# A delta-rule recurrence with a hardswish MLP behind it: eleven quarter products from block four on, and loads spread one a unit

## The chip, the cores and the metric

One core of a Trainium2 chip runs the whole kernel. The metric is the device time of one execution in microseconds (us). Five engines work side by side on the core: TensorE (PE, with its weight loads PEld), VectorE (DVE), ScalarE (ACT), GpSimd (POOL), and SyncE (SP), whose queue issues nearly all DMA transfers, in order, to the DMA engines. Each engine runs its own instructions in the order in which they were written and waits at semaphores for the others.

## The reference

Batch 4, 8 heads, 768 tokens, head width 48. A recurrence over the tokens (the delta rule) is followed by a two-layer MLP on 3072 tokens of width 384, with 2048 features in between:

```python
k_n = k / (np.linalg.norm(k, axis=-1, keepdims=True) + 1e-06)
for t in range(S):
    y[:, :, t] = q[:, :, t] @ state
    v_old = state^T @ k_n[:, :, t]
    state += beta[t] * outer(k_n[:, :, t], v[:, :, t] - v_old)
x = y.transpose(0, 2, 1, 3).reshape(B * S, H * D)
h = x @ w_in
g = h * np.clip(h + 3.0, 0.0, 6.0) / 6.0
out = g @ w_out
```

(the loop body is written here in short; all is float32).

## The kernel before

**The recurrence** is done in 24 chunks `t` of 32 tokens, for all batches and heads at once. For a chunk, `prep(t)` (from L505 on) scales the keys, turns keys and queries over on TensorE (`pt`, L524), evicts them into `KQ` (L532), and multiplies them with each other (`sc`, L547). The inverses of small triangular matrices are made in groups of four chunks on VectorE (L759 and L764). `chain(t)` multiplies with the state (`ks`, L806), then `pz` and `py` (L827) and the state's update `su` (L938), and hands the chunk's output over, turned (`yt`, L873, evicted to `xT` at L877). Keys go through `kf` (four chunks a tile, two tiles), queries through four buffers `qb`, values through two buffers `vf`. The norms of a group's keys need one square a chunk (`sq`, L409) and a reduction of it (L413).

**The MLP** works on blocks `blk` of two chunks, 256 rows, so there are twelve, 0 to 11. The up stage multiplies a block with `w_in`, the down stage the result `g` with `w_out`. `mlp_units` (L1286) gives the order: the down stage of a block, then the up stage of the next one. There are two ways to do an up stage. `up` (L982) does, for each of 16 groups of 128 features, three matmuls of 256 columns, which are twelve quarter products for each pair of groups (L994), followed by a relu on ACT (L1001) and a product on DVE (L1004). `up_by_eleven` (L1059) gets the eight quarter products of two thirds of the width from seven, by sums of weights and of tokens in the manner of Strassen and Winograd, and does the last third directly: eleven quarter products for a pair `j`, as nine matmuls (L1066) in `begin(j)` and `end(j)`. A pair also has an early eviction by ACT (L1080) with two additions on POOL (L1030), two on DVE (L1093 and L1097), a last copy (L1100), the relu (L1104) and the product (L1107). The relu writes into a tile named `o` that has one buffer. The down stage puts its results into the same `o`; from block 2 on it is `down_by_seven` (L1199, matmuls at L1218, sums of `g` at L1204, additions of results at L1228 on POOL and DVE). A block's results leave by eight stores (`to_dram`, L1143) on SP's queue.

`up_by_eleven` needs sums of `w_in` that are made once, in place of one part of it: `weight_sums` (L1032), sixteen operations on POOL, recorded two a step during the down stage of block `UF - 1`. It needs four sums of a block's tokens as well: `token_sums` (L1048), on DVE.

**The order.** A matmul in float32 leaves two records in the profile. The first chunks and the first units of the MLP follow an order written out by hand (`ORDER`; it holds the loads of chunks 0 to 11 of q, 0 to 16 of k and 0 to 5 of v). From chunk 5 on a loop does the rest: each chunk has 15 units, and in each unit come the pieces of `chain` and `prep` that `plan` names for it, then loads, then one unit of the MLP (`take(units)`), then a share of the inverses (`take(fill, ...)`). So two chunks hold the 14 units of a down stage and the 16 of an up stage; an up stage begins in unit 12 of an odd chunk. The loads of the loop are four of v at a chunk's start, four of q in its unit 2, and those of k (sixteen for four chunks), two a unit from the third chunk of a group on. `behind_tensor` (L1407) adds to an instruction a wait for the last TensorE instruction recorded so far; before, only words of `ORDER` use it.

Of the kernel before, what the change touches and what calls it, by code (L numbers as in the profile page):

```python
# [44 lines left out]
def kernel(  # L45
# [21 lines left out]
    nc = tc.nc  # L67
# [33 lines left out]
    def group(t):  # L101
        return (0, t) if t < G0 else ((t - G0) // GS + 1, (t - G0) % GS)
# [873 lines left out]
    def settle(n=0, name="u"):  # L976

        relu(name)
        while len(pending[name]) > n:
            pending[name].pop(0)()  # L980
# [34 lines left out]
                past.add(("up", blk))  # L1015
            yield

    UF = 5
    S1, S2, S4 = (sums_in[:, i] for i in range(3))

    def w_tiles(s, i):
# [10 lines left out]
    def weight_sums():  # L1032
        for j in range(0, NPR, 2):
            r = slice(j, j + 2)
            plus_minus(S1[:, r], W21[:, r], W22[:, r], ALU.add)
            yield
            plus_minus(S2[:, r], S1[:, r], W11[:, r], ALU.subtract)
            yield
            plus_minus(S4[:, r], W12[:, r], S2[:, r], ALU.subtract)
            yield  # L1040
            plus_minus(W21[:, r], W11[:, r], W21[:, r], ALU.subtract)
            yield
# [5 lines left out]
    def token_sums(blk):  # L1048
        if blk < UF or ("seam", blk * CB + 1) not in past:
            return  # L1050
        needs(("seam", blk * CB), ("seam", blk * CB + 1), ("up", blk - 1))
        B11, B12, B21, B22, _, _ = (
            x.rearrange("p (a b) -> p a b", b=16) for x in x_tiles(blk)
        )
        for out, a, b in ((T1x, B12, B11), (T2x, B22, T1x), (B12, B22, B12), (T4x, B21, T2x)):
            nc.vector.tensor_tensor(out=out, in0=a, in1=b, op=ALU.subtract)
        past.add(("sums", blk))
# [228 lines left out]
    def mlp_units():  # L1286
# [10 lines left out]
        def downs(blk):  # L1297
            if blk >= FIRST:
                yield from down_by_seven(blk)
                return  # L1300
            for c in range(CB):
                for f in range(0, NFC, WF):
                    if c == 0:
                        needs(*(("read", ("ph", blk, f + i, None)) for i in range(2)))
                    down(blk, c, f)
                    yield

        for blk in range(1, N // CB):
            mode["of"] = "down"
            mode["mean"] = 0.72 if blk + 1 < UF else 0.4  # L1310
            sums = weight_sums() if blk == UF - 1 else iter(())
            for _ in downs(blk):
# [3 lines left out]
            if blk + 1 < N // CB:  # L1316
                mode["of"] = "eleven" if blk + 1 >= UF else "up"
                for n, _ in enumerate((up_by_eleven if blk + 1 >= UF else up)(blk + 1)):
                    if blk + 1 == FIRST and n >= HF:
# [10 lines left out]
    def take(gen, n=1):  # L1330
        for _ in range(n):
            while next(gen, None) == 1:
                pass
# [6 lines left out]
    gens = {}  # L1340

    def made(name, make, ok=True):
        if name not in gens:
            gens[name] = make() if ok else iter(())
        return gens[name]

    def prep_of(t):
        return made(("p", t), lambda: prep(t), t < N)

    def chain_of(t):  # L1350
        return made(("h", t), lambda: chain(t))
# [4 lines left out]
    def inverse_of(g):  # L1356
        return made(
            ("i", g), lambda: halves_of(g) if g == 1 else inverse(g), g < NG
        )

    def keys_of(g):
        return made(
            ("k", g), lambda: chained(*(load_k(first(g) + i) for i in range(size(g)))), g < NG
        )
# [42 lines left out]
    def behind_tensor(ins):  # L1407
        last = next(
            i for i in reversed(nc.cur_bb.bb.instructions) if i.engine == mybir.EngineType.PE
        )  # L1410
        tc.add_manual_dep(
            ins, last.name,
            mybir.DependencyInfo(mybir.DependencyClass.Sync, mybir.DependencyReason.DATA),
            reason="held back",
        )

    def do(word):
        if word in ("K", "Q", "V", "W"):
            n = len(nc.cur_bb.bb.instructions)
            next(gens[word.lower()])  # L1420
            (new,) = nc.cur_bb.bb.instructions[n:]
            behind_tensor(new)
        elif word in gens:
            next(gens[word])
        elif word[0] == "r":
            relus[word[1]].pop(0)()
        elif word[0] == "g":
            pending[word[1]].pop(0)()
        elif word == "e":
            evicts.pop(0)()  # L1430
        elif word[0] == "i":
            next(inverse_of(int(word[1:])), None)
        else:
            name, t = word[0], int(word[1:])
            if name == "p" and t >= LS + LE:
                next(prep_of(t), None)
            else:
                key = (name, t) if name in "hp" else ("early", name, t)
                next(made(key, lambda: makers[name](t)), None)

    with tc.manual_schedule():
        for word in ORDER.split():
            word, _, n = word.partition("*")
            for _ in range(int(n or 1)):
                do(word)
        for name in relus:
            settle(0, name)
        while evicts:
            evicts.pop(0)()

        units = gens["u"]
        fill = inverse_of(2)
        loads = iter(())
        left = due = 0
        USED = {"up": 0.42, "eleven": 1.0, "down": 0.7}
        CHAIN = {0: 0.45, 1: 0.75, 2: 0.75, 3: 0.4, 4: 0.4, 6: 0.5, 9: 0.8, 10: 0.6, 14: 0.2}
        for t in range(LS, N):
            g, i = group(t)
            ch = chain_of(t)
            behind = t - LS < LA - LE  # L1460
            first_of = t + min(LA, LE + t - LS)
            now, more, later = (prep_of(first_of + n) for n in range(3))
            if not behind:
                more, later = (), more
            take(gens["v"], 4)
            if i == 0:
                left += 1
            if i == 2:
                loads = keys_of(g + 3)
            plan = {  # L1470
                0: lambda: take(ch),
                1: lambda: (take(ch), take(now)),
                2: lambda: (take(ch), take(now), take(gens["q"], 4)),
                3: lambda: take(ch),
                4: lambda: (take(ch), take(now)),
                5: lambda: take(now),
                6: lambda: take(now),
                8: lambda: take(ch),
                9: lambda: take(ch),
                10: lambda: take(ch),  # L1480
                11: lambda: token_sums(t // CB),
                13: lambda: take(later),
            }
            if behind:
                for u in (7, 8, 10, 11, 12, 13):
                    plan[u] = lambda ch=plan.get(u): (ch and u < 13 and ch(), take(more))
                plan[14] = lambda: take(later)
            ready = (2, 0) if behind or i == 2 and t - LS == LA - LE else (1, 6)
            for u in range(NU):
                if u in plan:  # L1490
                    plan[u]()
                take(loads, 2)
                if (i, u) == (0, 2):
                    drain(fill)
                    left = 0
                    fill = norms_of(g + 2)
                if (i, u) == ready:
                    drain(fill)
                    fill = inverse_of(g + 1)
                    take(fill)  # L1500
                    left, due = 2 * (C - 2) + 2, 0.0
                take(rest)
                take(gens["a"])
                take(units)
                settle(1)
                while evicts:
                    evicts.pop(0)()
                if i == 1 == ready[0] and 5 < u < 7:
                    continue
                if i == 0 or not left:  # L1510
                    take(fill, 2 if i or u < 2 else u > 4)
                    continue
                room = max(1.65 - USED[mode["of"]] - CHAIN.get(u, 0), 0.15) / mode["mean"]
                due += room * left / max((GS - i) * NU - u, 1)
                due = min(due, 2.6)
                take(fill, int(due))
                left, due = max(left - int(due), 0), due - int(due)
            drain(ch)
        for _ in units:
            settle(2)  # L1520
# [30 lines left out]
```

## Time and profile before

| what | value |
|---|---|
| median of 3 runs | 665.89 us (664.8 to 666.0) |
| the profiled execution, its own time | 665.93 us |
| its span, first to last instruction | 664.1 us |
| busy TensorE, 100 to 640 us | 539.3 of 540 us |
| chain that ended last, share of TensorE | 90% |
| transfers of q, k and v | 96 each, 48 KB, 2.2 to 2.8 us to landing |
| stores of results on SP | 92, 48 KB, 1.6 us to landing |

The span is what the instructions cover; the execution's own time is some 1.8 us longer. The share of an engine is over the whole span, so windows of single stages are read beside it. In a timeline a row gives start, duration, engine, line, operation, result and operands, and in brackets the time that the engine stood before it and what released it. A row of SP's queue is the issue of a transfer, not the transfer.

### The profile page before, as it was taken

How to read it: one execution, taken by the hardware profiler on the slowest of the kernel's cores; microseconds unless marked ns; L12 is line 12 of the kernel's file. 1: busy time of each engine (PE TensorE's matmuls, PEld its weight loads, DVE VectorE, ACT ScalarE, POOL GpSimd, SP SyncE). 2: the span in 40 equal slices, each digit the busy share in tenths (PEclk: the TensorE clock that was granted, in tenths of full speed). 3: DMA queues.
4: the chain of work that ended last, by engine and by line, in shares of the span. 5: the costliest groups of instructions: out<-in, count | busy, mean ns of one | idle time of the engine just before them, and what ended most of it. 6: DMA issues, size and time to landing. Idle time of an engine off the chain costs nothing.

```text
span 664.1 us, 26330 instructions
## 1 busy us (share of the span) xinstructions
PE 636.2 (96%) x11544; PEld 568.1 (86%) x11544; DVE 487.1 (73%) x1146; ACT 272.1 (41%) x532; POOL 203.5 (31%) x320
## 2 busy tenths in 40 slices
PE   2769999999999999999999999999999999999997
PEld 1658987776789989989989999999999999999997
DVE  4899867898555697657979748989658998456353
ACT  5897679331233143142144244244244144153350
POOL 6531112003511320562254354064052241331430
PEclk9659999999999999999999999999999999999999
DMA  7897246212140030041030030020020020000000
GB/s 175 206 236 197 76 98 161 49 28 41 23 83 8 10 66 3 2 85 27 2 74 3 2 74 3 3 61 2 3 50 2 2 50 1 23 19 2 25 1 25
DMA packets 88499, 33.27 MB, mean 50 GB/s; under 512 B 80160, under 2 KB 83232, under 8 KB 88384
## 3 DMA queue, kind: packets, MB, share of 16 engines
q1 hardware_dynamic: 88128, 31.29, 20.9%
q8 instruction: 91, 1.49, 0.9%
q10 hardware_dynamic: 256, 0.30, 0.2%
q14 instruction: 24, 0.20, 0.1%
HBM read 26.84 MB, written 4.72 MB: 48 GB/s over the span
## 4 chain that ended last, share of the span: by engine, by line
PE 90%; DVE 3%; DMA 2%; SPq 2%; ACT 1%; issue 1%; POOL 0%; ACTq 0%; DVEq 0%; POOLq 0%
PE po L1218 28%; PE ph L1066 20%; PE ph L994 16%; PE po L1154 6%; PE ks L806 3%; PE pt L524 3%; PE su L938 3%; PE pz L827 3%; PE py L827 3%; PE sc L547 3%; PE yt L873 1%; DMA spare<-in_moe_w_in_dram 1%; PE pi L684 1%; DMA w_out<-in_moe_w_in_dram 1%; SPq L168 1%
## 5 line engine op out<-in xcount | busy, mean ns | idle before, releaser
L1066 PE MATMUL ph<-xT,w_in 128*128 128x128 f32 (+1 forms) x560 | 121.4, 321 | 0.7 <-ACT KQ L532 0.5
L994 PE MATMUL ph<-xT,w_in 128*128 128x256 f32 (+1 forms) x576 | 117.1, 353 | 0.9 <-ACT xT L877 0.6
L1218 PE MATMUL po<-w_out,g 128*128 128x192 f32 x640 | 110.6, 326 | 0.0
L994 PEld LDWEIGHTS ph<-xT,w_in 128*128 128x128 f32 x576 | 95.2, 194 | 13.9 <-ACT xT L877 1.0
L1218 PEld LDWEIGHTS po<-w_out,g 128*128 128x128 f32 x640 | 104.6, 190 | 0.5
L1066 PEld LDWEIGHTS ph<-xT,w_in 128*128 128x128 f32 x560 | 91.1, 191 | 5.9 <-ACT KQ L532 0.7
L1030 POOL TENSOR_TENSOR g<-g 128x256 f32<-128x256 f32 x112 | 67.9, 608 | 83.2 <-ACT g L1080 78.8
L1218 PE MATMUL po<-spare,g 128*128 128x192 f32 x480 | 86.7, 332 | 0.0
L1218 PEld LDWEIGHTS po<-spare,g 128*128 128x128 f32 x480 | 77.2, 190 | 1.8
L1001 ACT ACTIVATE g<-ph,halves 128x256 f32<-128x256 f32 (+1 forms) x96 | 41.0, 436 | 74.2 <-PE ph L994 74.2
L1228 POOL TENSOR_TENSOR o<-o,u 128x192 f32<-128x192 f32 x18 | 13.2, 731 | 175.8 <-ACT o L1225 97.2
L1080 ACT ACTIVATE g<-ph 128x512 f32<-128x512 f32 x56 | 33.4, 597 | 81.8 <-PE ph L1066 81.8
L1204 DVE TENSOR_TENSOR g<-g 128x512 f32<-128x512 f32 x80 | 55.5, 715 | 5.6 <-PE po L1218 5.6
L759 DVE TENSOR_TENSOR pr<-A 128x30 f32<-128x30 f32 (+9 forms) x150 | 57.5, 383 | 2.7
L764 DVE TENSOR_TENSOR A<-A,pr 128x30 f32<-128x30 f32 (+9 forms) x150 | 55.7, 371 | 3.7
L1004 DVE SCALAR_TENSOR_TENSOR g<-g,ph 128x256 f32<-128x256 f32 (+1 forms) x96 | 34.7, 371 | 29.4 <-ACT g L1001 29.0
L356 ACT ACTIVATE spare<-spare,places 128x768 uint16<-128x768 uint16 (+1 forms) x56 | 52.6, 944 | 2.8 <-DMA kf<-in_k_dram 1.7
L1093 DVE TENSOR_TENSOR g<-ph,g 128x256 f32<-128x256 f32 x56 | 23.5, 420 | 38.5 <-PE ph L1066 30.9
L1225 ACT ACTIVATE o<-po 128x192 f32<-128x192 f32 x40 | 13.2, 330 | 83.2 <-PE po L1218 79.6
L1154 PE MATMUL po<-w_out,g 128*128 128x384 f32 x128 | 45.2, 491 | 0.0
L1107 DVE SCALAR_TENSOR_TENSOR g<-o,g 128x512 f32<-128x512 f32 x56 | 40.7, 726 | 5.9 <-ACT o L1104 5.9
L1104 ACT ACTIVATE o<-g,halves 128x512 f32<-128x512 f32 x56 | 40.4, 722 | 8.7 <-DVE g L1107 5.7
(141 smaller groups left out, 989.1 us busy)
## 6 DMA issues: line engine op xcount, KB each, us to landing
kf<-in_k_dram SPq DMA_DIRECT2D x96, 48.0 KB, 2.4
qb<-in_q_dram SPq DMA_DIRECT2D x96, 48.0 KB, 2.8
vf<-in_v_dram SPq DMA_DIRECT2D x96, 48.0 KB, 2.2
out_dram<-o SPq DMA_DIRECT2D x92, 48.0 KB, 1.6
spare<-in_moe_w_in_dram SPq DMA_DIRECT2D x4, 768.0 KB, 5.9
w_out<-in_moe_w_in_dram SPq DMA_DIRECT2D x4, 768.0 KB, 6.0
w_out<-in_moe_w_out_dram SPq DMA_DIRECT2D x4, 768.0 KB, 6.9
spare<-in_moe_w_out_dram SPq DMA_DIRECT2D x4, 768.0 KB, 5.0
```

What stands on the lines that cost most here:

```text
L356: nc.scalar.activation(out=z, in_=z if n else d.bitcast(I16)[:, :, :, 3], func=func, bias=places[:, n : n + 1], scale=scale,)
L759: nc.vector.tensor_tensor(out=pv, in0=A[:, j + 1 :, j].unsqueeze(2).to_broadcast([n, w, j]), in1=A[:, j, 0:j].unsqueeze(1).to_broadcast([n ...
L764: nc.vector.tensor_tensor(out=A[:, j + 1 :, 0:j], in0=A[:, j + 1 :, 0:j], in1=pv, op=ALU.subtract)
L994: nc.tensor.matmul(ph[:, cols], lhsT=w_in[:, s, f * 128 : (f + 1) * 128], rhs=xT[:, s, cols], start=(s == 0), stop=(s == NKT - 1),)
L1001: nc.scalar.activation(out=g, in_=ph, func=ACTF.Relu, bias=half, scale=1.0 / 6.0)
L1030: nc.gpsimd.tensor_tensor(out=out, in0=a, in1=b, op=op)
L1066: nc.tensor.matmul(ph[:, n], lhsT=w, rhs=x, start=start, stop=stop, skip_group_check=True)
L1104: nc.scalar.activation(out=r, in_=g, func=ACTF.Relu, bias=half, scale=1.0 / 6.0)
L1107: nc.vector.scalar_tensor_tensor(out=g, in0=r, scalar=1.0, in1=g, op0=ALU.min, op1=ALU.mult)
L1154: nc.tensor.matmul(pos[c][:], lhsT=gs[blk, f // 2][:, f % 2, c * P : (c + 1) * P], rhs=w_out[:, f, :], start=(f == 0), stop=(f == NFC - 1),)
L1204: nc.vector.tensor_tensor(out=A(f, *out, 4), in0=A(f, *a, 4), in1=A(f, *b, 4), op=op)
L1218: nc.tensor.matmul(ps[n][:], lhsT=A(f - f % 2, *a)[:, f % 2], rhs=b[:, f], start=(f == 0), stop=(f == HF - 1),)
```

## The change

`UF` goes from 5 to 4: block 4's product with `w_in` is done by `up_by_eleven` instead of `up`, the token sums begin with that block, and the weight sums are recorded in the down stage of block 3 instead of block 4. The loop's loads are recorded one a unit, in units 0 to 3 for v, 4 to 7 for q, and 8 to 14 for k, with one more of k in unit 7 of the third and fourth chunk of a group. Each gets a wait for the last TensorE instruction recorded before it.

```diff
-    UF = 5
+    UF = 4
...
+    def paced(gen):
+        n = len(nc.cur_bb.bb.instructions)
+        next(gen, None)
+        for new in nc.cur_bb.bb.instructions[n:]:
+            behind_tensor(new)
...
-            take(gens["v"], 4)
...
-                2: lambda: (take(ch), take(now), take(gens["q"], 4)),
+                2: lambda: (take(ch), take(now)),
...
-                take(loads, 2)
+                paced(gens["v"] if u < 4 else gens["q"] if u < 8 else loads)
+                if i in (2, 3) and u == 7:
+                    paced(loads)
```

The wait that `paced` adds comes from a function that was there before:

```python
    def behind_tensor(ins):
        last = next(
            i for i in reversed(nc.cur_bb.bb.instructions) if i.engine == mybir.EngineType.PE
        )
        tc.add_manual_dep(
            ins, last.name,
            mybir.DependencyInfo(mybir.DependencyClass.Sync, mybir.DependencyReason.DATA),
            reason="held back",
        )
```

## The prediction, made before the changed kernel ran

> **What bounds the kernel now.** I read the page's busy line and clock row first, then busy time by windows cut at block borders, then who waited for whom on TensorE, then the chain and the timelines around the one wait that this showed.
>
> ```profile
> PE 636.2 (96%) x11544; PEld 568.1 (86%) x11544; DVE 487.1 (73%) x1146; ACT 272.1 (41%) x532; POOL 203.5 (31%) x320
> PEclk9659999999999999999999999999999999999999
> ```
>
> TensorE is busy for 96% of the span. The missing time lies in the first 100 us and the tail, which the change does not touch. The windows below start at a block's first product and end at the next stage (columns: window, its length, busy us and instructions of PE, weight loads, DVE, ACT, POOL, granted clock, DMA share, GB/s).
>
> ```profile
> 257.21:281.52 24.31, 24.31 (x445) 23.24 (x444) 16.81 (x38) 5.09 (x12) 8.12 (x9) 1.00 0.01 3
> 281.52:308.35 26.83, 26.83 (x430) 23.03 (x428) 16.37 (x40) 9.56 (x20) 15.46 (x23) 1.00 0.36 69
> 332.65:359.10 26.45, 25.97 (x477) 23.44 (x476) 22.38 (x52) 12.82 (x26) 14.33 (x23) 1.00 0.24 48
> 383.41:409.40 25.99, 25.73 (x477) 23.56 (x476) 16.25 (x39) 12.93 (x26) 13.49 (x23) 1.00 0.24 49
> 433.71:459.47 25.76, 25.76 (x477) 23.41 (x476) 23.00 (x52) 12.92 (x26) 14.45 (x23) 1.00 0.20 41
> ```
>
> The first row is the down stage of block 3. Then come the up stages of blocks 4 (twelve quarter products), 5, 6 and 7 (eleven). Each holds the same recurrence work of two chunks beside its own products, so they can be compared. TensorE is full at clock 1.00 in all but two of them; the waits of TensorE from 100 us on name these two.
>
> ```profile
> PE ph L1066 <- ACT KQ L532: 0.5, 1, 0.5
> PE ph L1066 <- issue: 0.3, 1, 0.3
> ```
>
> So from 100 us on the end is set by the amount of TensorE work plus 0.7 us of waits. The larger wait is in block 5:
>
> ```profile
> 333.05 3.58 SPq L1143 DMA_DIRECT2D out_dram<-o  x8
> 336.21 2.79 DMA out_dram<-o
> 338.73 0.27 ACT L1100 ACTIVATE g<-ph 128x128 f32<-128x128 f32 x1
> 339.84 0.72 ACT L1104 ACTIVATE o<-g,halves 128x512 f32<-128x512 f32 x1 [0.83 <-ACT g L1100]
> 340.46 1.06 ACT L532 ACTIVATE KQ<-pt 128x512 f32<-128x512 f32 x2
> 341.10 0.49 PE L1066 MATMUL ph<-xT,w_in 128*128 128x128 f32 x2 [0.48 <-ACT KQ L532]
> ```
>
> These rows come from SP's timeline, the chain, and the timelines of ACT and PE. An eleven-product block puts its relu (L1104) into the one `o` buffer, so ACT must wait until the eight stores of the previous down stage have landed. Here the last store landed 2.8 us after its issue, L1104 started 0.8 us late, the KQ copy behind it on ACT was late, and TensorE stood 0.48 us. In block 7 the same L1104 starts 6.55 us after the block's first product with nothing late.
>
> **The change part by part.** (1) *Block 4 with eleven quarter products.* It removes 48 matmuls of 256 columns (two records each, 96) and adds 72 matmuls (144 records). Price from the windows: block 4 26.83, block 7 25.76, that is -1.07 us. A check without recurrence work around it is the last block:
>
> ```profile
> 622.66 19.47 PE ph L1066 x144
> ```
>
> Twelve products at the chain's "x12" pieces of 2.59 us come to 8 x 2.59 = 20.7; less 19.47 that is -1.25. Beside the recurrence a little is lost at each change of shape, so I take -1.07. The smallest gain that rows give is 26.83 - 25.99 (block 6) = -0.84. All of this lies on TensorE's path.
>
> (2) *Its evictions.* ACT loses 16 L1001 (0.44 us each) and gains 8 of L1080, L1100 and L1104 (0.60 + 0.27 + 0.72), +5.7 us. DVE loses 16 L1004 (0.42) and gains 8 x (0.41 + 0.29 + 0.73) and four token sums (0.49 + 0.63 + 0.67 + 0.28), +6.8 us. POOL gains 8 x 1.26 = 10.1 us. They are hidden behind TensorE: blocks 5 to 7 carry the same load with DVE at 16 to 23 us and POOL at 13 to 14 of 26. I cost them at nothing; without cover the bound is the wait in (3).
>
> (3) *The weight sums move one block earlier.* Sixteen POOL operations of 0.72 us leave the time of block 4 (285 to 304 us, and two more at 319) and go 51 us earlier, behind the up stage of block 3, where POOL idles 10 us at a stretch. Their last two stand in POOL's order behind the first `o` addition of the down stage, and now in front of four squares for the norms:
>
> ```profile
> 319.30 1.18 POOL L1030 TENSOR_TENSOR sums_in<-w_in,sums_in 128x256 f32<-128x256 f32 x1
> 320.44 0.87 POOL L1030 TENSOR_TENSOR w_in<-w_in 128x256 f32<-128x256 f32 x1
> 268.60 1.28 POOL L409 TENSOR_TENSOR sq<-kf 128x384 f32<-128x384 f32 x1
> 274.74 1.20 POOL L409 TENSOR_TENSOR sq<-kf 128x384 f32<-128x384 f32 x1 [0.67 <-DVE ss L413]
> 279.13 0.59 POOL L1228 TENSOR_TENSOR o<-o,u 128x192 f32<-128x192 f32 x1 [3.19 <-DVE u L1228]
> ```
>
> So the squares go up to 1.18 + 0.87 = 2.05 us later. POOL has 3.19 us of idle time before its next addition, but DVE, which reduces each square in order, has less: its addition into `u` (278.63 us) had waited only 0.71 us, so it can come up to 0.9 us later (the 2.05 less that wait, less about 0.4 made up in the pauses between the reductions, an estimate). The stores then start near 282.5 instead of 281.6. With 3.58 us for eight issues and 1.6 us for a landing (its median) the last has landed at 287.3; block 4's L1104 is due 6.55 us after 281.4, at 288.0. Cost: 0. Other end: eight issues took 5.16 us at 281.6, and the slowest landing in the window 332 to 340 was 3.3 us; this is the rival below.
>
> (4) *Loads one a unit, held to TensorE.* The same 48 KB loads, each now waiting for the last matmul before it. Queued behind it on SP are the next loads and the eight stores. A unit is some 1.7 us and an issue 0.45, so SP keeps up. A v or q load is used by the next chunk, about ten units or 17 us later, and lands in 2.2 to 2.8 us: covered. K loads are used five units or more after the last is issued. Only around block 5 do K loads stand before stores (five, then three behind): 5 x 0.45 = 2.25 us if they bunched; as the fifth waits for a product that ends before the last additions, I take 0. The stores of before have a burst of eight to sixteen loads behind them in the queue (vf right after each x8 row); with pacing it is thinned to one a unit. Whether that burst slowed the landing in block 5 the trace leaves open: behind block 7's stores it was the same, and all landed in 1.6 us. Bounds: 0 and the whole 0.48; I take -0.48, since in the other six such blocks no late store reaches TensorE.
>
> **Sum.** -1.07 (1) + 0 (2) + 0 (3) - 0.48 (4) = -1.55 us. The profiled execution took 665.93 us (span 664.1), within 0.1 us of the median of the runs, 665.89: 664.4. No more can come from waits than another 0.26, since TensorE has none left after 100 us.
>
> **A rule that speaks against it.** In one pair of 128-column records TensorE takes 0.22 us (starts 332.49, 332.71, 332.94), 0.11 a record, though its weight load has a row of 0.19 us: the loads hide behind the products before them. The Trainium skill ("TensorE: Matmul & The Clock Gate", Part 3, "The mechanism") says that a weight load overlaps matmuls in flight only if it goes to other row groups; all loads here use all 128 rows. With its load time of P/1.2 ns ("LDWEIGHTS"), 107 ns, an estimate for 48 more loads is 5.1 us, and the sum would be about +4. The trace disagrees, in seven blocks.
>
> **The rivals.**
> *The stall stays or moves to block 4 (18%).* For it: the slow landing need not come from the burst, and block 4 is now the first with this buffer conflict. Against: in four of the seven blocks L1104 is on time, and in two (0.5 and 0.4 us late) TensorE feels nothing. With one stall left, wherever, the sum is -1.07; with one in each block, 26.83 - 26.45 = -0.38 for block 4 and nothing for block 5: 664.9 to 665.6.
> *Late stores in block 4, slower (15%).* Place: POOL, then SP, then ACT's L1104. All 2.05 us pass through, the eight issues take 5.16 and the last landing 3.3: stores start at 283.7, the last is issued at 288.4 and landed at 291.7; L1104 is 3.7 us late. ACT has 0.3 us of slack (0.8 late gave 0.48), so TensorE stands 3.4 us: -1.07 + 3.4 = +2.3, 668.3. It decides from 1.4 us of lateness on (no gain). Against: POOL's idle 3.19 us, and it needs the slowest of every row.
> *Pacing clears block 6 as well (5%).* The 0.26 us "issue" wait falls during a burst of q loads; -1.55 - 0.26 and up to 0.3 from (1)'s upper end: 663.8 to 664.1, with run scatter 663.2.
> *Weight loads exposed (1%).* 48 more loads of 0.19 us: +9.2 - 1.1, 674. This is the rule above as rows price it.
> My forecast keeps 61%.
>
> **How the numbers follow.** A measurement of this kernel tells about 0.2%, 1.3 us, from no change. The forecast's own range is 663.6 to 664.9, on both sides of 664.56 where faster begins: 52 of its 61 parts faster, 9 within. Moved stall: 2 faster, 16 within. Late stores: 11 slower, 4 within. Block 6: 5 faster. Exposed loads: 1 slower. Together 0.59, 0.29, 0.12. The range 663.2 to 666.0 leaves out most of the late stores (14 in 100) and some 5 below.
>
> **What would show it.** Right: the window of block 4's up stage near 25.8 to 26.0 us with 144 records, block 5's near 25.8 with L1104 directly behind L1100, SP issuing a load every 1.7 us. Step 3 is wrong if block 4's L1104 carries a wait on `out_dram`, step 4 if block 5's still does. The whole is wrong if TensorE shows a new wait on a load or an eviction.

## The result, and the profile after

The changed kernel takes 669.85 us (median of 7 runs, 668.45 to 673.5), the kernel before 665.82 us (7 runs, 664.51 to 666.06). The ratio is 1.0053, with a 95% interval of 1.0032 to 1.0074: slower, by some 3.5 us by the ratio and 4.0 us between the medians, where 664.4 had been forecast. The profiled execution took 668.91 us (span 667.2). The page of the changed kernel, its busy line, its clock row and one row of its DMA queues:

```profile
PE 635.8 (95%) x11592; PEld 568.9 (85%) x11592; DVE 496.6 (74%) x1158; ACT 276.9 (42%) x540; POOL 215.1 (32%) x336
...
PEclk9968999999999999999999999999999999999999
...
q8 instruction: 91, 1.49, 0.9%
```

TensorE is 0.4 us less busy than before although it does less in block 4 alone by a whole microsecond, and the span is 3.1 us longer. The same five stages as in the prediction, by windows (window, length, busy us and instructions of PE, weight loads, DVE, ACT, POOL, clock, DMA share, GB/s):

```profile
258.23:282.64 24.41, 24.41 (x444) 23.18 (x443) 19.43 (x44) 5.09 (x12) 9.10 (x10) 1.00 0.13 25
282.64:308.96 26.32, 25.85 (x477) 23.52 (x476) 16.69 (x41) 12.82 (x26) 14.21 (x24) 1.00 0.15 33
333.27:360.70 27.43, 25.99 (x477) 23.49 (x477) 23.75 (x54) 12.93 (x26) 14.26 (x23) 1.00 0.21 44
385.01:410.59 25.58, 25.58 (x477) 23.49 (x477) 16.39 (x39) 12.93 (x26) 13.54 (x23) 1.00 0.15 34
434.96:461.49 26.53, 26.17 (x477) 23.47 (x476) 21.98 (x53) 12.82 (x26) 14.40 (x23) 1.00 0.15 32
```

Block 4's up stage (second row) does its work in 25.85 us, 0.98 less than before: the eleven products save what they should. But 0.47 us of waiting is added to it, block 5 (third row) has become 0.98 longer, and block 7 (last) 0.77 longer. TensorE's waits from 100 us on:

```profile
PE sc L547 <- issue: 1.4, 1, 1.4
PE ph L1066 <- ACT KQ L532: 0.8, 2, 0.5
```

The first is new, and the largest. It stands in the chain that ended last, in chunk 12's part of block 5:

```profile
343.82 0.81 PE pz L827 x64
344.63 0.69 PE sc L547 x47
345.32 1.44 issue
346.76 0.33 PE sc L547 x11
347.09 1.98 PE ph L1066 x15
```

In the kernel before, the chain passes the same two groups without a break:

```profile
343.79 0.81 PE pz L827 x64
344.60 0.79 PE sc L547 x53
```

In the changed kernel TensorE stops in the middle of a group of like matmuls. They have one line and one tile, the ones before the gap ran, and "issue" says that no engine and no transfer released them. What was missing were the instructions. The queue named "instruction" in the page moved 91 packets of 1.49 MB, 16,384 bytes each, for TensorE's 11,592 + 11,592 records and the 187 rows of its sequencer: 257 a packet. So TensorE's program comes in blocks of 256. With the first instruction counted as 0, the one that waited is number 13,249, which is 51 x 256 + 193; the 0.26 us "issue" wait of the kernel before stood at number 15,041, which is 58 x 256 + 193. In the seventeen profiles of this study TensorE has 47 waits of 0.2 us or more from 24 us on that are put down to "issue", and all 47 have the remainder 193: a block's first instruction. (Below, the place of an instruction is this remainder plus one, as the recorded expectations count it. So a block begins at place 194, and an instruction at place 215 is the 22nd of its block.)

The trace shows when the packet moved: 344.48 to 345.42 us, and TensorE went on 1.34 us after that. It also shows why it was late. Line 827 of the kernel before, and then of the changed kernel, between 338 and 344 us (the wait of TensorE's sequencer is "PEldq EVENT_SEMAPHORE"; count, duration in ns, first and last start):

```profile
L827 PE MATMUL pz<-R,X x25: 201/201/225, 343.7 to 344.0; 32*32 32x48 f32 x25
L827 PEldq EVENT_SEMAPHORE  x1: 51/51/51, 342.4 to 342.4; - x1
```

```profile
L827 PE MATMUL pz<-R,X x23: 201/201/225, 343.7 to 344.0; 32*32 32x48 f32 x23
L827 PEldq EVENT_SEMAPHORE  x1: 51/51/51, 343.2 to 343.2; - x1
```

The sequencer runs ahead of the matmuls. Before `pz` it waits for VectorE's `R`, until 342.4 before and 343.2 after, while TensorE is still busy with matmuls handed to it earlier: this wait costs nothing by itself and is in no list of TensorE's idle time. In the changed kernel `pz` is at place 215, and the packet of the next block had not started when the sequencer stood there. After the wait come 256 of the shortest instructions of the kernel (`pz` and `sc`, 1.6 us); the packet starts 1.2 us after the wait's end, moves for 0.9 us, is of use 1.3 us later, and is needed 235 instructions into the run. In the kernel before, `pz` is at place 114. The border that falls into its two groups (number 12,993) had its packet at 337.0 to 338.6 us, well ahead of the wait, and the packet of number 13,249 came at 345.2 to 346.3 us and was needed at 350.4. The 101 instructions between the two places are block 4's: 24 more matmuls of four instructions (two weight loads and two passes), and waits.

The Trainium skill ("Runtime: NRT & Kernel Launch", "Instruction fetch mechanics") says that instructions come in 16 KiB blocks of 256, that the sequencer asks for the next one by itself, and that crossing a border is mostly hidden. The trace agrees on the size, and on "mostly": past 110 us one border of 72 showed a gap of over 0.2 us in the changed kernel. Where the section says that the pace of issue hides the fetch, the 1.44 us are a place where it did not.

### The profile page after: what moved, and what is told of

Same layout as the page of the kernel before. It is cut to its first block, busy times and chain, and to the rows that moved or that the text cites. A ratio compares the mean times of both kernels' runs of the same rounds, so it can differ in the third digit from the quotient of the medians.

```text
span 667.2 us, 26615 instructions
## 1 busy us (share of the span) xinstructions
PE 635.8 (95%) x11592; PEld 568.9 (85%) x11592; DVE 496.6 (74%) x1158; ACT 276.9 (42%) x540; POOL 215.1 (32%) x336
## 3 DMA queue, kind: packets, MB, share of 16 engines
q8 instruction: 91, 1.49, 0.9%
## 4 chain that ended last, share of the span: by engine, by line
PE 87%; DMA 3%; DVE 3%; ACT 2%; SPq 2%; issue 1%; POOL 0%; ACTq 0%; DVEq 0%; POOLq 0%
PE po L1218 28%; PE ph L1066 23%; PE ph L994 11%; PE po L1154 6%; PE ks L806 3%; PE pt L524 3%; PE su L938 3%; PE pz L827 3%; PE py L827 3%; PE sc L547 2%; PE yt L873 1%; ACT spare L356 1%; DMA w_out<-in_moe_w_in_dram 1%; DMA spare<-in_moe_w_in_dram 1%; SPq L168 1%
## 5 line engine op out<-in xcount | busy, mean ns | idle before, releaser
L1066 PE MATMUL ph<-xT,w_in 128*128 128x128 f32 (+1 forms) x640 | 138.9, 321 | 0.8 <-ACT KQ L532 0.8
L1066 PEld LDWEIGHTS ph<-xT,w_in 128*128 128x128 f32 x640 | 104.1, 191 | 7.2 <-ACT KQ L532 1.3
L1030 POOL TENSOR_TENSOR g<-g 128x256 f32<-128x256 f32 (+1 forms) x128 | 77.4, 606 | 96.6 <-ACT g L1080 91.6
L994 PE MATMUL ph<-xT,w_in 128*128 128x256 f32 (+1 forms) x480 | 94.9, 348 | 0.7 <-ACT xT L877 0.6
L994 PEld LDWEIGHTS ph<-xT,w_in 128*128 128x128 f32 x480 | 77.9, 196 | 10.7 <-ACT xT L877 1.0
L1080 ACT ACTIVATE g<-ph 128x512 f32<-128x512 f32 x64 | 38.2, 597 | 95.8 <-PE ph L1066 95.8
L1093 DVE TENSOR_TENSOR g<-ph,g 128x256 f32<-128x256 f32 x64 | 26.8, 419 | 45.3 <-PE ph L1066 39.5
L1001 ACT ACTIVATE g<-ph,halves 128x256 f32<-128x256 f32 (+1 forms) x80 | 33.7, 429 | 56.2 <-PE ph L994 56.1
L1107 DVE SCALAR_TENSOR_TENSOR g<-o,g 128x512 f32<-128x512 f32 x64 | 47.3, 739 | 6.8 <-ACT o L1104 6.8
L1104 ACT ACTIVATE o<-g,halves 128x512 f32<-128x512 f32 x64 | 46.2, 722 | 10.6 <-DVE g L1107 7.1
L1066 PE MATMUL ph<-beta_tok,sums_in 128*128 128x128 f32 x256 | 49.5, 275 | 0.0
```

What stands on the lines that cost most here:

```text
L994: nc.tensor.matmul(ph[:, cols], lhsT=w_in[:, s, f * 128 : (f + 1) * 128], rhs=xT[:, s, cols], start=(s == 0), stop=(s == NKT - 1),)
L1030: nc.gpsimd.tensor_tensor(out=out, in0=a, in1=b, op=op)
L1066: nc.tensor.matmul(ph[:, n], lhsT=w, rhs=x, start=start, stop=stop, skip_group_check=True)
L1104: nc.scalar.activation(out=r, in_=g, func=ACTF.Relu, bias=half, scale=1.0 / 6.0)
L1107: nc.vector.scalar_tensor_tensor(out=g, in0=r, scalar=1.0, in1=g, op0=ALU.min, op1=ALU.mult)
```

## The experiments

Of every run the profile gives the length of the stages, first product to next stage, and the time from block 2's first up product to TensorE's end. These were read off the timelines of TensorE:

```
us                           b3 up  b3 down  b4 up  b5 up  b6 up  b7 up  block 2 to end
before                       26.83   24.31   26.83  26.45  25.99  25.76      483.1
changed                      27.10   24.41   26.32  27.43  25.58  26.53      484.3
changed, again               27.09   24.41   25.92  27.41  25.58  26.26      483.6
eleven alone                 27.10   24.43   25.91  29.41  25.57  26.29      485.9
pacing alone                 26.83   24.31   26.82  26.14  25.75  25.75      482.5
spread without wait          27.08   24.42   26.54  27.88  25.58  26.66      485.1
waits in bursts              27.08   24.43   26.02  27.42  25.58  26.51      484.3
before, 100 more (chunk 10)  26.83   24.31   27.81  27.91  25.58  26.34      485.7
before, 100 more (chunk 12)  26.83   24.30   26.83  27.48  25.57  26.69      484.6
changed, 44 more (chunk 10)  27.08   24.42   26.54  25.76  26.72  25.92      483.9
changed, 44 more (chunk 12)  27.10   24.42   26.44  27.90  26.80  25.76      485.6
unit ahead of pz             27.11   24.43   26.72  26.53  25.58  26.70      484.4
as well, sums held           26.83   30.87   25.58  26.60  25.58  26.80      489.3
44 more, relu's own tile     27.09   24.41   26.04  25.75  25.57  25.82      481.7
before, relu's own tile      26.83   24.31   26.83  25.69  26.29  25.75      482.6
```

The time ahead of block 2 differs from one profiled execution to the next by more than the whole effect (block 2 starts at 175.9 to 181.0 us, and the kernel before without an edit ran from 664.5 to 674.0 us over the chips used), so the table is read for single stages, and the ratios for the whole. Where matmuls were added, a stage holds them too: 0.63 us for 100 instructions, 0.28 for 44.

### The two parts of the change apart

*Eleven products in block 4 alone* (`UF = 4` in the kernel before, nothing else):

> The eleven quarter products in block 4 alone (UF = 4), the loads recorded as before. Theory 'pacing costs': the 3.5 us loss comes from the loads held to TensorE, so this kernel is faster than before by about the work saved, 0.5 to 1.1 us: ratio 0.9983 to 0.9993. Theory 'block 4 costs': the earlier weight sums and the fuller VectorE lose more than the product saves: ratio 1.003 to 1.007, as the whole change.

*The pacing alone* (the change without `UF = 4`):

> The loads one a unit with their waits for TensorE, block 4 with twelve products as before. 'Pacing costs': ratio 1.006 to 1.008 (3.5 us and the 0.5 to 1.1 us that the products save). 'Block 4 costs': ratio within 0.001 of 1.

*The change with the loads spread but not held to TensorE:*

```diff
         for new in nc.cur_bb.bb.instructions[n:]:
-            behind_tensor(new)
+            pass
```

> The whole change without the waits for TensorE: the loads are recorded one a unit, but SP may run ahead. 'Pacing costs by the waits or by the time at which the loads then run': ratio about 0.998 to 0.999. 'Pacing costs by the order on the queue': ratio 1.003 or more, as the whole change. 'Block 4 costs': 1.003 to 1.007.

*The change with the loads held to TensorE but in their old bursts:*

```diff
-            take(gens["v"], 4)
+            for _ in range(4):
+                paced(gens["v"])
```

(and q and k in the same way)

> The whole change with the loads at their old places in the program (four v at a chunk's start, four q in unit 2, two k a unit), each with a wait for TensorE. If the cost is in the waits themselves (more semaphore updates by TensorE, more instructions on SP) or in loads that run throughout a block rather than behind the stores, it stays: ratio 1.003 or more. If it is in the spreading to one a unit, it goes: 0.998 to 0.999.

Measured, as ratios to the kernel before: eleven alone 1.0018 [1.0003, 1.0033], pacing alone 1.0000 [0.9988, 1.0011], spread without wait 1.0020 [1.0004, 1.0036], waits in bursts 1.0014 [0.9998, 1.0030]. The pacing alone neither gains nor costs. The three kernels with eleven products in block 4 lose some, the third not beyond its interval. But they lose less than the 1.003 to 1.007 that the theory 'block 4 costs' had foreseen, and about a third of the whole change's 1.0053; why the whole change loses more than any part of it is not shown. TensorE's waits in the three with eleven products have one row in common. Eleven alone, then spread without wait, then waits in bursts:

```profile
PE sc L547 <- issue: 1.9, 1, 1.9
```

```profile
PE sc L547 <- issue: 1.9, 1, 1.9
PE ph L1066 <- ACT KQ L532: 1.2, 2, 0.7
```

```profile
PE sc L547 <- issue: 1.4, 1, 1.4
PE ph L1066 <- ACT KQ L532: 0.4, 2, 0.3
```

In the run with eleven alone the gap had an aftermath (windows, columns as above):

```profile
349.00:351.20 2.20, 1.56 (x22) 1.47 (x22) 1.13 (x4) 0.11 (x1) 0.00 (x0) 0.98 0.40 75
351.20:354.60 3.40, 3.40 (x14) 3.04 (x14) 0.59 (x2) 1.38 (x3) 1.96 (x3) 0.51 0.00 0
354.60:358.00 3.40, 3.40 (x131) 2.96 (x134) 3.30 (x8) 1.49 (x3) 1.19 (x2) 1.00 0.00 0
```

After the pause the granted clock is 0.51 for 3.4 us, which is another 1.7 us lost, and then 1.00 again. The changed kernel's own profile, with a shorter gap, does not show it, and neither does that of the spread loads, whose gap was as long (1.90 us). So this loss comes in some executions and not in others.

### Is it the place in the block?

If so, 100 instructions that nobody needs must bring the gap into the kernel before, and 44 must take it out of the changed one. They are copies of the state update's matmuls into columns of its bank that are never read:

```diff
+            for n in range(25 if t == 10 else 0):
+                h, b = n % H, n // H
+                nc.tensor.matmul(
+                    su[b // 2][DP * (h % 2) : DP * (h % 2) + DP, b % 2, NP * D : NP * D + D],
+                    lhsT=bkb[rows(b), h], rhs=Z[rows(b), D * h : D * h + D],
...
```

*The changed kernel again, for comparison on one chip:*

> The changed kernel once more, for the other runs of this group to be set against on one chip. Both theories: slower than before, ratio 1.001 to 1.006; a gap of 1.4 to 2.1 us put down to 'issue' at L547 in block 5's first product, since every kernel with eleven products in block 4 has shown it there.

*The kernel before, 100 more in chunk 10* (as shown):

> The kernel before with 25 more matmuls (100 TensorE instructions, 0.63 us by the su rows) whose results nobody reads, at the end of chunk 10's state update. Theory 'blocks': TensorE's instructions come in blocks of 256, the next block is asked for only when its sequencer has passed the wait ahead of pz, and with eleven products in block 4 pz of chunk 12 stands at instruction 215 of a block, ahead of 256 short instructions. The extra 100 put it at 214 here too, with block 4 as it was: a gap put down to 'issue' at L547 of about 0.8 us (the wait ends 1.28 us ahead of pz here, 0.50 us in the changed kernel), and the 0.26 us gap of block 6 gone; the span longer by 0.63 + 0.8 - 0.26 = 1.2 us, ratio 1.0017. Theory 'block 4': the loss comes from the eleven products' own sums and additions, which this kernel does not have there: no gap, longer by the 0.63 us of the extra matmuls, ratio 1.0009.

*The changed kernel, 44 more in chunk 10* (`11 if t == 10`):

> The changed kernel with 11 more such matmuls (44 instructions, 0.28 us) at the end of chunk 10's state update, so that pz of chunk 12 stands at instruction 3 of the next block. Theory 'blocks': no gap at L547 in block 5; the first product of block 5 takes 25.7 to 26.1 us in place of 27.4, and the whole 1.1 to 1.6 us less than the changed kernel: ratio to the kernel before 0.998 to 1.001. Theory 'block 4': the gap stays, ratio as the changed kernel's or 0.0004 above.

*The changed kernel, 44 more in chunk 12* (`11 if t == 12`):

> The changed kernel with the same 11 matmuls two chunks later, at the end of chunk 12's state update, behind the place of the gap. Theory 'blocks': pz of chunk 12 is at 215 as in the changed kernel, so the gap of 1.4 to 2.1 us is there; from chunk 13 on it is the run with 44 more at chunk 10 instruction for instruction, so the difference between the two is the gap: 1.4 us or more, 0.002 of the ratio. Theory 'the extra matmuls help by something else': the same time as that run.

*The kernel before, 100 more in chunk 12* (`25 if t == 12`, run later):

> The kernel before with the same 100 extra instructions as in the run that had them in chunk 10, but in chunk 12, behind its pz, which stays at 114 of its block. Theory 'blocks': no gap at L547 in block 5; longer than the kernel before by the 0.63 us of the extra matmuls alone, less the 0.26 us of block 6, ratio 1.0005 to 1.0015, against 1.0065 [1.0047, 1.0083] with them in chunk 10. Rival 'the extra matmuls cost more than their 0.63 us wherever they stand': ratio 1.003 or more, gap or not.

Ratios: the change again 1.0047 [1.0028, 1.0066]; before with 100 more 1.0065 [1.0047, 1.0083]; changed with 44 more in chunk 10 1.0007 [0.9988, 1.0026], in chunk 12 1.0040 [1.0025, 1.0054]; before with 100 more in chunk 12 1.0018 [0.9997, 1.0038]. The kernel before, with block 4 as it always was, now has the gap in the chain, at the same group:

```profile
347.67 0.81 PE pz L827 x64
348.49 0.70 PE sc L547 x48
349.19 1.46 issue
350.66 0.33 PE sc L547 x10
```

The changed kernel with 44 instructions in front does the two groups without a break, and block 5's up stage as a whole (a window) holds no wait:

```profile
343.88 0.81 PE pz L827 x64
344.69 0.79 PE sc L547 x53
345.48 1.53 PE ph L1074 x12
```

```profile
333.33:359.09 25.76, 25.76 (x476) 23.40 (x476) 23.66 (x54) 12.93 (x26) 14.30 (x23) 1.00 0.24 48
```

(with the added lines, L1074 is L1066.) With the same 44 two chunks later the gap is there, 1.6 us. So the gap follows the place of `pz`, in either kernel, and not the eleven products. Most of the loss in time goes with it: the ratio falls from 1.0047 to 1.0007 with the 44 ahead of the place, and stays at 1.0040 with the same 44 behind it. The time of `KQ` waits that came up in block 6 (0.87 us) is in the 1.0007.

The kernel before with the 100 in chunk 12 has no "issue" wait past 100 us, as the theory said. Its ratio does not decide, since the interval holds both forecasts: its profile is 1.5 us longer from block 2 on, 0.63 of it the extra matmuls, and TensorE waits for `KQ` in blocks 5 and 7 (0.60 and 0.49 us).

What the traces show of the one block, number 13,249 on:

```
us                           pz at   wait for R over   packet starts   landed   TensorE goes on
changed                       215        343.25           344.48       345.42       346.76
changed, again                215        343.28           344.42       345.35       346.77
eleven alone                  215        345.63           347.16       348.04       349.64
before, 100 more (chunk 10)   214        346.56           347.77       349.35       350.66
spread without wait           215        342.00           343.73       344.68       345.98
waits in bursts               215        341.57           342.71       343.78       345.08
changed, 44 more (chunk 12)   215        342.65           343.74       345.04       346.35
changed, 44 more (chunk 10)     3        343.31           339.94       340.81       no gap
```

In the seven runs with a gap the packet starts 1.1 to 1.7 us after the wait is over, and TensorE goes on 1.3 to 1.6 us after it has landed.

Two things are not settled. The ratio 1.0065, 4.3 us, is more than the 1.2 us expected, and more than the 2.6 us that its profile has from block 2 on. That profile has another 3.1 us ahead of block 2, where nothing was changed.

And what decides whether a wait holds the next block back was not found; the place alone does not. Place 226 was passed in three runs; 231 held in one run and not in another, where the packet started 1.1 us before the wait was over. In the kernel before, `pz` of chunk 11 is at 214 with no harm. Its packet started 1.6 us before the wait was over, although in the run with 100 more the same place held. So the sequencer's stand at the wait explains these seven runs, but it is not a full account of when a block is asked for.

### Can the gain of block 4 be had?

*One unit of block 5's products ahead of chunk 12's `pz`,* which moves `pz` to 231 with no instruction added:

```diff
+                if (t, u) == (12, 4):
+                    take(units)
                 if u in plan:
                     plan[u]()
...
-                take(units)
+                if (t, u) != (12, 4):
+                    take(units)
```

> The changed kernel with no instruction added: in chunk 12 one unit of block 5's quarter products is issued ahead of pz and not behind it, so that pz stands at instruction 231 of its block of 256 in place of 215. Theory 'blocks': the sequencer passes the point where the next block is asked for ahead of its wait for R (226 was passed ahead, 214 and 215 not), so no gap at L547 in block 5, block 5's first product 25.7 to 26.3 us, ratio to the kernel before 0.9985 to 1.0015. Rival 'only the extra matmuls helped': gap and time as in the changed kernel, ratio 1.003 or more.

*As well, the weight sums held behind TensorE:*

```diff
-                next(sums, None)
-                next(sums, None)
+                for _ in range(2):
+                    n = len(nc.cur_bb.bb.instructions)
+                    next(sums, None)
+                    for new in nc.cur_bb.bb.instructions[n:]:
+                        behind_tensor(new)
```

> As the run with the unit ahead of pz, and GpSimd's 24 weight sums each wait for the TensorE instruction issued before them, so that they run during block 3's second product and not ahead of it, during its first. Theory 'GpSimd's sums slow VectorE's chain operations': block 3's first product is back at 26.83 us (27.1 with the sums run ahead), its second at 24.31 to 24.45; 0.3 us less than the run without the hold. Rival 'the 0.27 us is from something else': first product still 27.1.

*As well, the relu in the pair's own PSUM bank:*

```diff
-                ro = mlp.tile([128, CB, DM], FP32, name="o", bufs=1)
-                r = ro[:].rearrange("p c m -> p (c m)")[:, 0 : 2 * TB]
+                r = ph[:].rearrange("p i c -> p (i c)")
```

(the bank is given free after VectorE's product and not after the last copy)

> As the run with the sums held, and the Relu of a pair of quarter products goes into the pair's own PSUM bank and not into the tile that the stores of the block before are read from, so ScalarE does not wait for those stores (0.25 to 0.96 us of TensorE waiting for KQ behind it). Theory 'the rest of the lost gain is that wait': no wait of TensorE for KQ in blocks 4 to 7, ratio to the kernel before 0.997 to 0.9985. Rival: the bank is held one unit longer, and TensorE waits for a bank instead: ratio 1.000 or more.

*That one with eleven products from block 3 on* (`UF = 3`, two units ahead of chunk 8's `pz`):

> As the run with the Relu in the bank, but eleven products from block 3 on, the weight sums one block earlier again, and two units ahead of pz in chunk 8 (pz at 228) in place of the one in chunk 12 (pz at 52). Theory 'each block with eleven products is worth 1.07 us when the waits are out of the way': block 3's first product 25.8 us and not 26.8, 0.8 to 1.1 us less than the run from block 4 on. Rival 'the sums meet the end of the regular start': a wait of TensorE or VectorE in block 2, no gain.

Ratios: 1.0010 [0.9995, 1.0024], 1.0093 [1.0074, 1.0112], 1.0611 [1.0575, 1.0647], 1.0509 [1.0484, 1.0535]. The unit ahead of `pz` removes the gap, and the ratio is within the forecast. Block 5's up stage takes 26.53 us all the same, not the 25.7 to 26.3 foreseen, since TensorE waits 0.7 us for a late `y` there; blocks 4 and 7 keep waits for `KQ` of 0.87 and 0.48 us. The hold settles one point: block 3's up stage is back at 26.83 us, so the 0.27 us there came from the sums running ahead. (There are sixteen of them, not the 24 of the expectation.) But they then push the squares for the norms (L409) back, VectorE waits for these with `y` in line behind them, and TensorE stands in the next stage, which takes 30.87 us where 24.31 to 24.45 had been foreseen:

```profile
PE yt L873 <- DVE y L863: 4.0, 1, 4.0
PE pz L827 <- DVE X L473: 0.8, 1, 0.8
PE sc L547 <- issue: 0.8, 1, 0.8
```

(The 0.8 us of "issue" is block 5's gap again, with `pz` at place 231.) The relu in the bank was a bad exchange. TensorE waits for the bank now, on VectorE's first addition (L1105), nineteen times:

```profile
PE ph L1066 <- DVE g L1105: 20.8, 19, 1.9
```

The last kernel of the four inherits it (24 such waits, 25.3 us) and tells nothing of eleven products in block 3.

*A tile of its own for the relu* asks for room; the queries give it, with three buffers and not four. First in the changed kernel with 44 more instructions in chunk 10, then in the kernel before:

```diff
-    NKB, NQB, NBKB, NLB, NKQ, NVY = 2, 4, 8, 7, 6, 2
+    NKB, NQB, NBKB, NLB, NKQ, NVY = 2, 3, 8, 7, 6, 2
...
-                ro = mlp.tile([128, CB, DM], FP32, name="o", bufs=1)
-                r = ro[:].rearrange("p c m -> p (c m)")[:, 0 : 2 * TB]
+                r = mlp.tile([128, 2 * TB], FP32, name="r", bufs=1)[:]
```

> The changed kernel with the 44 more instructions in chunk 10 (no gap in block 5 there), and the Relu of a pair of quarter products in a tile of its own, for which the queries have three buffers and not four. Theory 'the stores': what is left of the loss is ScalarE's wait for the block before's stores, which it shares a tile with; no wait of ScalarE for out_dram at the Relu line and none over 0.3 us of TensorE for KQ in blocks 4 to 7, end from block 2's start on 1 us shorter than with the 44 alone (483.9 us there, 483.1 in the kernel before), ratio 0.9975 to 0.9995. Rival 'queries with three buffers come late': waits of VectorE or GpSimd for qb, no gain.

> The kernel before with the Relu in a tile of its own and three query buffers, to tell what of the run above is the eleven products in block 4 and what is the tile. Theory 'the stores': its one wait for KQ of 0.48 us in block 5 goes, ratio 0.999 to 0.9998, and the run above is 0.3 to 0.8 us less than this one. Rival 'block 4 with eleven gains nothing': the two within 0.2 us, or this one the faster.

Ratios 0.9990 [0.9968, 1.0011] and 0.9981 [0.9957, 1.0006]: neither is shown to be faster than the kernel before, nor one than the other; the medians even have the kernel with twelve products in block 4 ahead, 666.36 us to 667.47. The profiles show the mechanism all the same. In the first, TensorE waits for nothing from 100 us to the end, and ScalarE never for `out_dram` at the relu. Its blocks 4 to 7 by windows:

```profile
281.55:307.59 26.04, 26.04 (x499) 23.95 (x499) 16.73 (x40) 12.93 (x26) 14.04 (x24) 1.00 0.16 33
331.89:357.64 25.75, 25.75 (x477) 23.42 (x476) 23.64 (x54) 12.93 (x26) 14.25 (x23) 1.00 0.24 48
382.07:407.64 25.57, 25.57 (x476) 23.48 (x476) 16.37 (x39) 12.92 (x26) 13.52 (x23) 1.00 0.16 34
431.95:457.77 25.82, 25.82 (x477) 23.59 (x476) 22.97 (x53) 12.93 (x26) 14.39 (x23) 1.00 0.16 33
```

Block 4 takes 26.04 us with 22 records of the added matmuls (0.28 us, an estimate from the 0.63 us of 100 instructions), so its own are 25.76, and 26.83 less 25.76 is 1.07. From block 2 on it needs 481.7 us against 482.6 with twelve products in block 4 and the same tile, and 483.1 in the kernel before. Not all of the 0.9 us between the two is the eleven products' doing. The kernel with twelve has lost its wait for `KQ`, but in block 6 it still stands at the border 15,041, and that stage takes 26.29 us and not 25.57:

```profile
395.05 0.27 PE L1066 MATMUL ph<-xT,w_in 128*128 128x128 f32 x1 [0.55 <-issue]
```

Without these 0.72 us, and without the 0.28 us of matmuls added to the other kernel, some 0.5 us are left (an estimate): the 1.07 of block 4 less the 0.36 that block 3 has become longer, and some 0.2 in other stages. That is less than the intervals of these ratios can tell (0.2%, 1.4 us, to either side).

## Why the prediction was wrong

**The step that failed is the sum:** "No more can come from waits than another 0.26, since TensorE has none left after 100 us." It took the waits of before for the only ones, put new ones at nothing, and let TensorE's end move with TensorE's work. The change puts 101 instructions into TensorE's stream in block 4; everything behind them takes another place in its blocks of 256, and in block 5 a border fell where 256 short instructions follow a late wait: 1.44 us in the profiled execution, 1.4 to 1.9 in others. New waits for the stores (0.83 us) and the slower block 3 (0.37 us) came to it; they are under (3). The "issue" wait in block 6 of before was this same thing at a milder place. I read it as something that a burst of loads might cause; the number of its instruction would have told otherwise. It went in the changed kernel, whose `pz` of chunk 14 moved from 175 to 20: the third rival's 0.26 us came about, though not by pacing.

**(1) Eleven products, -1.07:** right. 25.85 us of work in the changed kernel's block 4, and by the estimate above 1.07 less where the waits were out of the way.

**(2) Evictions at nothing:** right, as far as the traces show. The wait for `R` does end only 0.50 us ahead of `pz` in block 5 and no longer 1.28, but not because VectorE is later: `R` is done 9.90 us after the stage's first product before and 9.94 after. `pz` comes earlier in the stage, at 10.48 us and not 11.22, mostly because 0.48 us of waiting for `KQ` ahead of it is gone. The kernel before with the relu in a tile of its own has the same short lead, 0.53 us, with `pz` at place 114, and no gap.

**(3) Weight sums a block earlier, 0:** wrong by 0.37 us. The sums do not stay in the down stage where they are recorded; GpSimd runs ahead and does fourteen of the sixteen during block 3's up stage. There VectorE's operations of the inverses become slower. The groups of VectorE in that stage, before and then after:

```profile
L764 DVE TENSOR_TENSOR A<-A,pr 128x198 f32<-128x198 f32 (+8 forms) x16 | 7.8, 487 | 0.6
```

```profile
L764 DVE TENSOR_TENSOR A<-A,pr 128x198 f32<-128x198 f32 (+8 forms) x16 | 9.7, 608 | 0.6
```

608 ns for 487; with the sums held back it was 436. So `y` is late for `yt`, 27.10 us for 26.83, and 0.10 in the down stage. The rival of late stores in block 4 came true in small: the stores started 1.2 us into the up stage, as worked out (1.1), but eight issues took 4.81 us and not 3.58, and the relu waited. ScalarE in the changed kernel's block 4:

```profile
288.88 0.27 ACT L1100 ACTIVATE g<-ph 128x128 f32<-128x128 f32 x1
289.98 0.72 ACT L1104 ACTIVATE o<-g,halves 128x512 f32<-128x512 f32 x1 [0.82 <-DMA out_dram<-o]
290.60 1.06 ACT L532 ACTIVATE KQ<-pt 128x512 f32<-128x512 f32 x2
```

That cost TensorE 0.47 us of the 3.4 priced. A wait of the same kind (TensorE for `KQ`) cost 0.36 more in block 7, and both differed from run to run.

**(4) Pacing, -0.48:** wrong. Alone it is worth nothing that can be measured (1.0000), though in its profile block 5's wait is 0.18 us for 0.48. With the whole change the wait left block 5 and came up in blocks 4 and 7; the first rival had named block 4. What removed it was a tile of its own.

**The account.** From block 2 on, the changed kernel's profiled execution is longer by 1.2 us: +0.37 in block 3, -0.51 in block 4 (-0.98 and +0.47), +0.98 in block 5 (1.44 more, 0.48 less), -0.41 in block 6, +0.77 in block 7. Another 0.9 us is ahead of block 2, where nothing was changed and where single executions differ by more, and 0.9 us lies behind TensorE's last product (4.67 us to the end, 3.80 before). The second profile of the changed kernel has the same gap and the same block 3, less waiting in blocks 4 and 7, and is only 0.5 us longer than before from block 2 on. So the waits named here are shown, but they do not add up to the measured loss of 3.5 to 4.0 us. That most of it goes with the gap is shown by the ratios of the two runs with 44 more instructions; how a gap of 1.4 us comes to cost so much is not, and the three kernels with a part of the change had the gap too and lost a third. That the half clock after the gap, seen after one gap of 1.9 us and not after the other, makes up the rest is possible and was not shown.

The weight-load rule that spoke against the change did not show: 1.07 us were saved with 48 more records.

## What to carry to other kernels

When TensorE is full, an edit that only adds or removes instructions also moves every later border of its instruction blocks; before it is called a gain, look for long groups of short matmuls behind a wait that ends late, and count where they stand. An "issue" gap in the middle of a like group is to be looked at by its instruction's number, and a few idle instructions or a unit moved ahead test it cheaply. A measured loss can also hide a right idea: take the change apart by stages before it is dropped.

## What the runs showed of the hardware

- TensorE's instructions arrive 256 at a time: in seven runs a packet of 16,384 bytes moved for 0.9 to 1.6 us, and where TensorE had run out, the first instruction of the block ran 1.3 to 1.6 us after it had landed. In these runs the packet did not start while the sequencer stood at its wait: from the wait's end to the new block's first instruction 3.5 to 4.1 us passed.
- The "issue" gaps ahead of block 2, up to 2.8 us at number 1473, lie at such borders too; they are part of why one execution differs from the next.
- After one gap, put down as 1.9 us, the granted clock was 0.51 for 3.4 us; after another of 1.90 us it stayed at 1.00. The Trainium skill ("TensorE: Matmul & The Clock Gate", Part 1, "What's actually happening") names an idle window of about 3.4 us for the half clock and a busy one of about 3.4 us for the full clock; the length of the slow stretch agrees with the second, and the pause before it was shorter than the first.
- GpSimd's work made VectorE's slower: with fourteen of the weight sums on GpSimd beside them, sixteen operations of the inverses took 608 ns each, against 487 in the kernel before and 436 with the additions held back.
